# A gated attention and expert kernel: another order for the lead-in, dummy matmuls, ten halved units, and one copy on VectorE

## The chip, the cores and the metric

The kernel runs on one core of one Trainium2 chip. The metric is the device time of one execution in microseconds (us). Before the change it is 1477.9 us, the median of three runs (1477.68 to 1480.69). The engines are named TensorE (PE; its weight loads PEld), VectorE (DVE, in the code V), ScalarE (ACT, A), GpSimd (POOL, G) and SyncE (SP), which issues most transfers (DMAs).

## What is computed

A linear recurrence with a complex decay per head, then a mixture of four experts, then a two-layer block. With q, k, v, a_re, a_im of shape 4 x 8 x 768 x 48:

```
a      = (a_re, a_im) * min(|a|, 0.999) / (|a| + 1e-6)
S[t]   = a[t] * S[t-1] + k[t] v[t]^T          (complex S, 48 x 48 per head)
y[t]   = q[t] . Re S[t]
x      = y of all heads side by side           (3072 tokens x 384)
x      = sum_e p_e * (relu(x @ w1[e]) @ w2[e])  (4 experts, 384 -> 1024 -> 384)
out    = leaky_relu(x @ w_in, 0.01) @ w_out     (384 -> 2048 -> 384)
```

## The kernel before

**Chunks.** The 3072 tokens are 24 chunks of 128. For each chunk the recurrence is done in closed form. `elementwise(c)` is a generator of 17 steps on VectorE, ScalarE and GpSimd: clip, logarithms, a running sum of log magnitudes (scan), the decays, a running sum of phases (scan), its reduction, sine and cosine, and at last the features `ft` of q and k. An eighteenth call runs `by_head`, six transfers that rearrange `ft` into `hd` by head. `products(c)` is a generator on TensorE: transposes of k into `kt` (two steps, each with a copy out of PSUM), scores `sc` with the causal mask on VectorE (two steps), the state update `pm` / `st`, the output `py` in two steps of four heads with the copy `y`, and the transposes `px` of y with the split of the result into a rounded part `xh` and a rest `xl`. All of these use two PSUM buffers in turn (`ps_a`).

**Groups and units.** Four chunks are a group of 512 tokens, six groups in all. A unit is a slice of 128 hidden columns: 32 units of the experts (first stage), 16 of the last block (second stage). For each step of the list `order`, `gemm_in` does nine matmuls into `ph`, VectorE makes `hp` of it, ScalarE rounds it to `hh`, VectorE takes the rest `hl` (`split_h`), and `gemm_out` does nine matmuls into three sums `acc`. `gemm_in` runs two steps ahead of `gemm_out`. Weights of the first stage come as `raw`, are split into rounded part and rest by ScalarE and GpSimd (`split_unit`; for the first three units by `cast_early` and, on TensorE, `rest_early`), stored to memory (`ws`, L626), and loaded back for later groups (`load_split`). The second stage's weights are decoded in the background.

**Halves.** In the first group the first `NHALF` units run twice in half width: first all of them for the first 256 tokens (chunks 0 and 1), then all of them for the other 256 (chunks 2 and 3), so that matmuls can begin when two chunks are ready. A half step has 256-column matmuls.

**What sets the order.** Each engine works its instructions off in the order in which the program lists them, and so does SP with its transfers. Up to the first `gemm_in` the string `PLAN` (L35) is that order: a digit is one step of `elementwise` of that chunk, `p` and `q` are steps of `products` of chunks 0 and 1, `s` an early cast, `m` an early rest, `n` the normalised probabilities. After it `background()` (L531) lists what is left, one *tick* at a time: the rest of `elementwise` of chunks 2 and 3, `WAIT` empty ticks, `products` of chunk 2 and of chunk 3, then for each later chunk `NSTEPS` ticks, those in `PSTEPS` being steps of its `products` and the others steps of the next chunk's `elementwise`. `tick` (L581) is called twice in each step, after `gemm_in` and after `gemm_out`, and takes as many ticks as the table `pace` asks for, at most three a call. `pace` goes from 0 at the start to `first` ticks at `KN` units, and then evenly to the beginning of each group, less `MARGIN`.

**The end of a stage.** `evacuate` (L600) copies the three sums to `o`, all on ScalarE, behind the `hh` of the step after next. The first matmuls of the next `gemm_out` write the same three sums.

Of the kernel before, what the change touches and what calls it, by code (L numbers as in the profile page):

```python
# [10 lines left out]
F32 = mybir.dt.float32  # L11
# [8 lines left out]
P = 128  # L20
# [4 lines left out]
NG = DM // P  # L25
DG = 16
TG = 512
# [3 lines left out]
NU = 48  # L31
WU = 2 * DM
AR_MIN = 0.76
NHALF = 8
PLAN = (  # L35
    "0101001010101011" "01ss0000mm" "00sss11mm000" "1111ppsm23111qq"
    "23232n3pp23p2ppqq3q23qqpq23m"
)
MAXT = 3
KN = 3.0  # L40
PT = 32
TPOOL = 6
MARGIN = 2.0
LAG = 2
E2 = 20
RAWS = 4
WTS = 7
DEC = 33.0
PSTEPS = (1, 3, 5, 12, 14, 17, 20, 22, 24)
ESTEPS = 17  # L50
LOADSTEP = 9
NSTEPS = ESTEPS + len(PSTEPS)
WAIT = 4
AR_MAX = 1e4
AI_MAX = 1.0
PI = 3.1415925
# [5 lines left out]
def fused_kernel(  # L62
# [13 lines left out]
    V, A, G, SP, PE = nc.vector, nc.scalar, nc.gpsimd, nc.sync, nc.tensor  # L76
# [6 lines left out]
    with ExitStack() as fast:  # L83
# [74 lines left out]
        def table(name):  # L158
            if tables[0] != name:
                A.preload_act_table_set(name)  # L160
                tables[0] = name

        def elementwise(c):
            t, vt = inputs[c]
            ar, ai, q, k = (t[:, i] for i in range(4))
# [77 lines left out]
        def by_head(c):  # L243

            ft, vt = feats[c]
            pool = p_el2 if c in (1, 3) else p_el
            hd = pool.tile([2 * D, H, 2 * P + 1], F32, name="hd")
            for ri in range(2):
                for i in range(NG):
                    row = ri * D + i * DG  # L250
                    (A if c < 2 and (i == ri or i == 2 - ri) else SP).dma_start(hd[row : row + DG], ft[:, ri, i])
            feats[c] = (ft, hd, vt)


# [3 lines left out]
        def products(c):  # L258
            if c >= CPG:
                by_head(c)  # L260
                yield
            ft, hd, vt = feats.pop(c)
            pool = p_el2 if c in (1, 3) else p_at
            first = c % NCH == 0
            kt = pool.tile([P, H, 2 * D], F32, name="kt", bufs=1)
            for ri in range(2):
                pt = ps_a.tile([P, NG, P], F32, name="pt", tag="pa")
                for i in range(NG):
                    PE.transpose(pt[:, i], ft[:, ri, i, P : 2 * P], ident)  # L269
                A.copy(  # L270
                    kt[:, :, ri * D : (ri + 1) * D].rearrange("t h (r d) -> t r d h", d=DG),
                    pt.rearrange("t r (d h) -> t r d h", h=H),
                )
                yield
            att = pool.tile([P, H, P], F32, name="att", bufs=1)
            for hh in range(2):
                sc = ps_a.tile([P, 4, P], F32, name="sc", tag="pa")
                for j in range(4):
                    h = 4 * hh + j
                    PE.matmul(sc[:, j], hd[:, h, P : 2 * P], hd[:, h, :P], start=True, stop=True)  # L280
                V.tensor_tensor(
                    att[:, 4 * hh : 4 * hh + 4], sc, causal[:, None].to_broadcast([P, 4, P]), ALU.mult
                )
                yield
            old = state.pop(c, None)
            if (c + 1) % NCH:
                pm = ps_a.tile([2 * D, H, D], F32, name="pm", tag="pa")
                for h in range(H):
                    PE.matmul(pm[:, h], kt[:, h], vt[:, h * D : (h + 1) * D], start=True, stop=True)  # L289
                st = p_at.tile([2 * D, H, D], F32, name="st")  # L290
                decay = hd[:, :, 2 * P :].to_broadcast([2 * D, H, D])
                if first:
                    V.tensor_tensor(st, pm, decay, ALU.mult)
                else:
                    V.tensor_tensor(st, pm, old, ALU.add)
                    V.tensor_tensor(st, st, decay, ALU.mult)
                state[c + 1] = st
                yield
            py = ps_a.tile([P, H, D], F32, name="py", tag="pa")
            for h in range(H):  # L300
                PE.matmul(py[:, h], att[:, h], vt[:, h * D : (h + 1) * D], start=True, stop=first)  # L301
                if not first:
                    PE.matmul(py[:, h], hd[:, h, :P], old[:, h], start=False, stop=True)  # L303
                if h == 3:
                    yield
            y = pool.tile([P, DM], F32, name="y", bufs=1)
            A.copy(y, py.rearrange("t h e -> t (h e)"))
            yield
            px = ps_a.tile([P, NG, P], F32, name="px", tag="pa")
            for i in range(NG):  # L310
                PE.transpose(px[:, i], y[:, i * P : (i + 1) * P], ident)  # L311
            grp, j = divmod(c, CPG)
            if j == 0:
                xg[grp] = (
                    p_x.tile([P, NG, TG], F32R, name="xh"),
                    p_x.tile([P, NG, TG], F32R, name="xl"),
                )
            xh, xl = (x[:, :, j * P : (j + 1) * P] for x in xg[grp])
            A.copy(xh, px)
            V.tensor_tensor(xl, px, xh.bitcast(F32), ALU.subtract)  # L320
            yield
# [164 lines left out]
                PE.matmul(out, wt[:, 0, cols], hl, start=False, stop=last)  # L486


        def zipped(*gens):
            gens = list(gens)  # L490
            while gens:
                for x in list(gens):
                    if next(x, gens) is gens:
                        gens.remove(x)
                yield

        def run_all(*gens):
            gens = list(gens)
            while gens:
                gens = [x for x in gens if next(x, gens) is not gens]  # L500

        with tc.manual_schedule():
            table("natural_log_exp_and_others")
            load_chunk(0, 0)
# [9 lines left out]
            steps = {str(c): elementwise(c) for c in range(CPG)}  # L514
            steps.update(zip("pqrt", (products(c) for c in range(CPG))))
            early_halves = iter([(s, part) for s in range(6) for part in (0, 1)][: PLAN.count("s")])
            for x in PLAN + "m" * 8:
                if x in steps:
                    next(steps[x], None)
                elif x == "n":  # L520
                    normalise_probs()
                    load_pb(0)
                elif x == "s":
                    cast_early(*next(early_halves))
                elif x == "m":
                    rest_early()
            for s in (5, 6):
                load_unit(s)
            split_unit(3, 0)

            def background():  # L531
                for _ in range(2):
                    next(steps["2"])
                    yield
                for _ in zipped(steps["2"], steps["3"]):
                    yield
                load_chunk(4)
                for _ in range(WAIT):
# [32 lines left out]

            dec = decoding()

            first = 2 + max(0, ESTEPS + 1 - min(PLAN.count("2"), PLAN.count("3"))) + WAIT + E2 - PLAN.count("r") - PLAN.count("t")
            pace = [(0.0, 0), (KN, first)]
            for g in range(1, NGRP):
                pace.append((begins[g] - MARGIN, first + ESTEPS + (NSTEPS + 1) * CPG * g))
# [22 lines left out]
            def evacuate(acc):  # L600

                out = [pools["x2"].tile([P, TG], F32, name="o", bufs=NG) for _ in acc]
                for o, a in zip(out, acc):
                    A.copy(o, a)  # L604
                return out

            acc = None
# [235 lines left out]
```

## Time and profile before

| what | value |
|---|---|
| median of three runs | 1477.9 us |
| the profiled execution | 1478.36 us |
| its span | 1476.6 us |
| TensorE busy | 1402.4 us, 95% |
| VectorE busy | 864.7 us, 59% |
| ScalarE busy | 564.8 us, 38% |
| mean granted clock of TensorE over the execution | 0.976 |

The profile records one execution. Busy time is the time in which an engine had an instruction at work. The granted clock is 1.0 for TensorE's full clock and 0.5 for half. In lists in order of time, the bracket at the end of a line gives the idle time of the engine before it and what ended that time.

### The profile page before, as it was taken

The page shows a single profiled execution, that of the slowest core. Times are in us where ns is not written, and L with a number is a line of the kernel's source. Part 1 is how long each engine was busy: PE and PEld are TensorE (multiplying, and loading weights), DVE is VectorE, ACT ScalarE, POOL GpSimd, SP SyncE. Part 2 cuts the span into 40 slices and gives each one's busy share as a digit, 9 for nine tenths or more (in the row PEclk, how much of TensorE's full clock was granted, in tenths as well). Part 3 has the DMA queues.
Part 4 walks back from the last instruction along what each step waited for, and adds up shares of the span by engine and source line. Part 5 has one row for each costly group of instructions (what it writes and reads, how often), then busy time and mean ns, then how long its engine had stood idle before and what let it go on. Part 6 is the DMA issues. An engine that isn't in the chain of part 4 may idle for free.

```text
span 1476.6 us, 18540 instructions
## 1 busy us (share of the span) xinstructions
PE 1402.4 (95%) x6978; PEld 1177.2 (80%) x6978; DVE 864.7 (59%) x1504; ACT 564.8 (38%) x961; POOL 264.5 (18%) x244
## 2 busy tenths in 40 slices
PE   3858999999999999999999999999999999999997
PEld 1858888888777888788888888888888888888886
DVE  7556887788988898785454554554443333333332
ACT  5424565444345434455234354233332111323232
POOL 2120565412223223221011110110110000100000
PEclk9569999999999999999999999999999999999999
DMA  7288789986788789588567477576465665556561
GB/s 192 43 207 301 212 255 298 331 291 208 273 301 290 250 305 319 153 303 245 153 234 222 151 242 216 188 222 199 154 199 172 231 207 196 190 188 208 190 212 65
DMA packets 91043, 325.49 MB, mean 220 GB/s; under 512 B 10464, under 2 KB 32064, under 8 KB 90944
## 3 DMA queue, kind: packets, MB, share of 16 engines
q1 hardware_dynamic: 87488, 318.71, 67.1%
q10 hardware_dynamic: 3456, 5.51, 1.3%
q8 instruction: 56, 0.92, 0.3%
q14 instruction: 43, 0.35, 0.1%
HBM read 262.72 MB, written 42.52 MB: 207 GB/s over the span
## 4 chain that ended last, share of the span: by engine, by line
PE 58%; DVE 2%; ACT 0%; issue 0%; DVEq 0%; ACTq 0%
PE ph L455 27%; PE acc L484 9%; PE acc L486 9%; PE acc L485 9%; PE sc L280 1%; PE py L301 1%; PE py L303 1%; PE pm L289 1%; PE pt L269 0%; DVE hl L473 0%; DVE hp L460 0%; PE px L311 0%; DVE d L349 0%; ACT hh L472 0%; DVE d L355 0%
## 5 line engine op out<-in xcount | busy, mean ns | idle before, releaser
L455 PE MATMUL ph<-xh,wt 128*128 128x512 f32 (+1 forms) x1200 | 397.9, 388 | 0.0
L484 PE MATMUL acc<-hh,wt 128*128 128x512 f32 (+1 forms) x888 | 350.8, 395 | 5.2 <-ACT o L604 5.1
L486 PE MATMUL acc<-hl,wt 128*128 128x512 f32 (+1 forms) x888 | 342.9, 386 | 4.5 <-DVE hl L473 4.5
L485 PE MATMUL acc<-hh,wt 128*128 128x512 f32 (+1 forms) x888 | 341.5, 385 | 0.0
L472 ACT CAST hh<-hp 128x512 fp32r<-128x512 f32 (+1 forms) x296 | 180.4, 610 | 418.2 <-DVE hp L460 326.5
L473 DVE TENSOR_TENSOR hl<-hp,hh 128x512 fp32r<-128x512 f32 (+1 forms) x296 | 213.4, 721 | 150.3 <-ACT hh L472 149.1
L455 PEld LDWEIGHTS ph<-xh,wt 128*128 128x128 f32 x1200 | 225.5, 190 | 42.4 <-ACT ge L121 0.3
L460 DVE SCALAR_TENSOR_TENSOR hp<-ph,pb 128x512 f32<-128x512 f32 (+1 forms) x200 | 133.0, 665 | 189.9 <-PE ph L455 188.6
L455 PE MATMUL ph<-xl,wt 128*128 128x512 f32 (+1 forms) x600 | 230.2, 384 | 0.0
L486 PEld LDWEIGHTS acc<-hl,wt 128*128 128x128 f32 x888 | 167.3, 188 | 40.0 <-DVE hl L473 6.0
L455 PE MATMUL ph<-x2h,wt 128*128 128x512 f32 x576 | 198.3, 398 | 0.0
L484 PEld LDWEIGHTS acc<-hh,wt 128*128 128x128 f32 x888 | 167.7, 189 | 36.5 <-ACT o L604 5.8
L485 PEld LDWEIGHTS acc<-hh,wt 128*128 128x128 f32 x888 | 168.0, 189 | 30.7
L463 DVE SCALAR_TENSOR_TENSOR hp<-hp 128x512 f32<-128x512 f32 x96 | 72.0, 750 | 185.0 <-ACT hp L462 184.9
L455 PEld LDWEIGHTS ph<-xl,wt 128*128 128x128 f32 x600 | 114.1, 190 | 20.3 <-DVE xl L320 0.2
L455 PEld LDWEIGHTS ph<-x2h,wt 128*128 128x128 f32 x576 | 108.7, 189 | 25.1
L462 ACT COPY hp<-ph 128x512 f32<-128x512 f32 x96 | 56.3, 586 | 178.5 <-PE ph L455 178.5
L455 PE MATMUL ph<-x2l,wt 128*128 128x512 f32 x288 | 114.5, 397 | 0.0
L409 POOL TENSOR_TENSOR wt<-raw,wt 128x384 fp32r<-128x384 f32 x58 | 65.0, 1142 | 62.4 <-ACT wt L408 62.3
L643 POOL TENSOR_TENSOR x2l<-o,x2h 128x512 fp32r<-128x512 f32 x18 | 25.2, 1424 | 256.4 <-ACT x2h L642 256.4
L301 PE MATMUL py<-vt,att 128*128 128x48 f32 x384 | 70.9, 280 | 0.1
L280 PEld LDWEIGHTS sc<-hd 96*128 96x128 f32 x384 | 54.2, 208 | 15.4 <-issue 7.9
(97 smaller groups left out, 1482.2 us busy)
## 6 DMA issues: line engine op xcount, KB each, us to landing
wt<-ws_scratch SPq DMA_DIRECT2D x264, 768.0 KB, 4.8
ws_scratch<-wt SPq DMA_DIRECT2D x32, 768.0 KB, 7.5
hd<-ft SPq DMA_DIRECT2D x138, 128.5 KB, 5.4
aaqk<-in_attn_dram SPq DMA_DIRECT2D x22, 768.0 KB, 8.9
raw<-in_w_dram SPq DMA_DIRECT2D x32, 384.0 KB, 4.5
r<-in_w_dram SPq DMA_DIRECT2D x32, 384.0 KB, 7.4
ws_scratch<-dw SPq DMA_DIRECT2D x32, 384.0 KB, 6.2
pb<-pn_scratch SPq DMA_DIRECT2D x24, 256.0 KB, 6.5
```

Source lines behind the costliest of these rows:

```text
L280: PE.matmul(sc[:, j], hd[:, h, P : 2 * P], hd[:, h, :P], start=True, stop=True)
L301: PE.matmul(py[:, h], att[:, h], vt[:, h * D : (h + 1) * D], start=True, stop=first)
L409: G.tensor_tensor(wt[:, 1], raw, wt[:, 0].bitcast(F32), ALU.subtract)
L455: PE.matmul(ph[:, : t1 - t0], wt[:, wi, cols], x[kc][:, t0:t1], start=n == 0, stop=n == 3 * NG - 1)
L460: V.scalar_tensor_tensor(hp, ph, 0.0, pbs[g, u // 8][:, t0:t1], ALU.max, ALU.mult)
L462: A.copy(hp, ph)
L463: V.scalar_tensor_tensor(hp, hp, 0.01, hp, ALU.mult, ALU.max)
L472: A.copy(hh, hp)
L473: V.tensor_tensor(hl, hp, hh.bitcast(F32), ALU.subtract)
L484: PE.matmul(out, wt[:, 0, cols], hh, start=first, stop=False)
L485: PE.matmul(out, wt[:, 1, cols], hh, start=False, stop=False)
L486: PE.matmul(out, wt[:, 0, cols], hl, start=False, stop=last)
```

## The change

`PLAN` has another order from its fourth part on, without the eight `m` at its end, and with the letter `w`: three dummy matmuls (`warm`) of 384 columns into the bank of the first sum, read by nobody. `products` of chunk 1 has four more dummies among the heads of `py`, and its `kt` is copied by VectorE. Chunk 1's `by_head` is issued by SP alone. `NHALF` is 10 for 8. The steps of chunks 2 and 3 that are left follow the string `LATER`, one to a tick, chunk 2 first; `WAIT` is 11, `KN` 4, and `first` follows from these (48 ticks, before 36). In `PSTEPS` the steps of `py` come one tick earlier and `px` one later, in the last tick of its chunk. In `evacuate` VectorE copies the middle sum.

```
--- before.py
+++ after.py
@@ -31,26 +31,27 @@
 NU = 48
 WU = 2 * DM
 AR_MIN = 0.76
-NHALF = 8
+NHALF = 10
 PLAN = (
-    "0101001010101011" "01ss0000mm" "00sss11mm000" "1111ppsm23111qq"
-    "23232n3pp23p2ppqq3q23qqpq23m"
+    "0101001010101011" "01ss0000mm" "00sss11mm000" "1111ppsmww23111"
+    "23n22qqw33ppm22p3ppmqqw3q2233qqpq"
 )
+LATER = "23222232232223333333"
 MAXT = 3
-KN = 3.0
+KN = 4.0
 PT = 32
 TPOOL = 6
 MARGIN = 2.0
 LAG = 2
-E2 = 20
+E2 = 17
 RAWS = 4
 WTS = 7
 DEC = 33.0
-PSTEPS = (1, 3, 5, 12, 14, 17, 20, 22, 24)
+PSTEPS = (1, 3, 5, 12, 14, 17, 19, 21, 25)
 ESTEPS = 17
 LOADSTEP = 9
 NSTEPS = ESTEPS + len(PSTEPS)
-WAIT = 4
+WAIT = 11
 AR_MAX = 1e4
 AI_MAX = 1.0
 PI = 3.1415925
@@ -160,6 +161,15 @@
                 A.preload_act_table_set(name)
                 tables[0] = name
 
+        def warm(n):
+
+            out = ps_acc.tile([P, TG], F32, name="warm", tag="acc0")
+            for _ in range(n):
+                PE.matmul(
+                    out[:, : NG * P], ident, inputs[0][0][:, 0].rearrange("p g t -> p (g t)"),
+                    start=True, stop=True,
+                )
+
         def elementwise(c):
             t, vt = inputs[c]
             ar, ai, q, k = (t[:, i] for i in range(4))
@@ -248,7 +258,7 @@
             for ri in range(2):
                 for i in range(NG):
                     row = ri * D + i * DG
-                    (A if c < 2 and (i == ri or i == 2 - ri) else SP).dma_start(hd[row : row + DG], ft[:, ri, i])
+                    (A if c == 0 and (i == ri or i == 2 - ri) else SP).dma_start(hd[row : row + DG], ft[:, ri, i])
             feats[c] = (ft, hd, vt)
 
 
@@ -267,7 +277,7 @@
                 pt = ps_a.tile([P, NG, P], F32, name="pt", tag="pa")
                 for i in range(NG):
                     PE.transpose(pt[:, i], ft[:, ri, i, P : 2 * P], ident)
-                A.copy(
+                (V.tensor_copy if c == 1 else A.copy)(
                     kt[:, :, ri * D : (ri + 1) * D].rearrange("t h (r d) -> t r d h", d=DG),
                     pt.rearrange("t r (d h) -> t r d h", h=H),
                 )
@@ -301,6 +311,8 @@
                 PE.matmul(py[:, h], att[:, h], vt[:, h * D : (h + 1) * D], start=True, stop=first)
                 if not first:
                     PE.matmul(py[:, h], hd[:, h, :P], old[:, h], start=False, stop=True)
+                if c == 1 and h % 2:
+                    warm(1)
                 if h == 3:
                     yield
             y = pool.tile([P, DM], F32, name="y", bufs=1)
@@ -486,19 +498,6 @@
                 PE.matmul(out, wt[:, 0, cols], hl, start=False, stop=last)
 
 
-        def zipped(*gens):
...
-        def run_all(*gens):
...
         with tc.manual_schedule():
             table("natural_log_exp_and_others")
             load_chunk(0, 0)
@@ -514,7 +513,7 @@
             steps = {str(c): elementwise(c) for c in range(CPG)}
             steps.update(zip("pqrt", (products(c) for c in range(CPG))))
             early_halves = iter([(s, part) for s in range(6) for part in (0, 1)][: PLAN.count("s")])
-            for x in PLAN + "m" * 8:
+            for x in PLAN:
                 if x in steps:
                     next(steps[x], None)
                 elif x == "n":
@@ -524,15 +523,15 @@
                     cast_early(*next(early_halves))
                 elif x == "m":
                     rest_early()
+                elif x == "w":
+                    warm(3)
             for s in (5, 6):
                 load_unit(s)
             split_unit(3, 0)
 
             def background():
-                for _ in range(2):
-                    next(steps["2"])
-                    yield
-                for _ in zipped(steps["2"], steps["3"]):
+                for x in LATER:
+                    next(steps[x], None)
                     yield
                 load_chunk(4)
                 for _ in range(WAIT):
@@ -571,7 +570,7 @@
 
             dec = decoding()
 
-            first = 2 + max(0, ESTEPS + 1 - min(PLAN.count("2"), PLAN.count("3"))) + WAIT + E2 - PLAN.count("r") - PLAN.count("t")
+            first = len(LATER) + WAIT + E2
             pace = [(0.0, 0), (KN, first)]
             for g in range(1, NGRP):
                 pace.append((begins[g] - MARGIN, first + ESTEPS + (NSTEPS + 1) * CPG * g))
@@ -600,8 +599,8 @@
             def evacuate(acc):
 
                 out = [pools["x2"].tile([P, TG], F32, name="o", bufs=NG) for _ in acc]
-                for o, a in zip(out, acc):
-                    A.copy(o, a)
+                for i, (o, a) in enumerate(zip(out, acc)):
+                    (V.tensor_copy if i == 1 else A.copy)(o, a)
                 return out
 
             acc = None
```

## Rows read from the trace of the kernel before

**Rows 1.** The profile page, its head.

```profile
span 1476.6 us, 18540 instructions
```

**Rows 2.** Busy time by stretches: us, then the columns of the head line.

```profile
core 0: us, PE busy (x) PEld busy (x) DVE busy (x) ACT busy (x) POOL busy (x), PEclk, DMA share, GB/s
...
44.47:66.66 22.19, 22.19 (x105) 21.04 (x106) 9.22 (x20) 4.06 (x8) 0.00 (x0) 0.50 0.08 30
...
66.74:128.01 61.27, 43.46 (x310) 42.00 (x309) 34.62 (x65) 20.99 (x41) 15.10 (x14) 0.81 0.75 225
...
128.01:285.00 156.99, 149.11 (x839) 127.69 (x838) 124.95 (x204) 86.97 (x156) 80.54 (x72) 0.99 0.87 268
...
320.00:600.00 280.00, 272.15 (x1391) 227.85 (x1390) 249.43 (x454) 120.99 (x204) 73.11 (x65) 1.00 0.81 279
```

**Rows 3.** TensorE in order of time: start us, us, engine, line, operation, tiles.

```profile
27.70 0.81 PE L429 MATMUL ph<-raw,ident 128*128 128x384 f32 x2
...
50.48 3.75 PE L280 MATMUL sc<-hd 96*128 96x128 f32 x16
...
54.02 2.69 PE L289 MATMUL pm<-vt,kt 128*96 128x48 f32 x16
...
66.74 0.58 PE L455 MATMUL ph<-xh,wt 128*128 128x256 f32 x1
...
95.70 0.55 PE L280 MATMUL sc<-hd 96*128 96x128 f32 x1 [5.40 <-DMA hd<-ft]
...
116.64 0.39 PE L301 MATMUL py<-vt,att 128*128 128x48 f32 x2
...
118.41 0.36 PE L455 MATMUL ph<-xh,wt 128*128 128x256 f32 x1
...
122.01 0.55 PE L311 MATMUL px<-ident,y 128*128 128x128 f32 x3 [0.57 <-ACT y L307]
...
125.85 0.28 PE L455 MATMUL ph<-xh,wt 128*128 128x256 f32 x1
...
128.01 0.28 PE L455 MATMUL ph<-xh,wt 128*128 128x256 f32 x1
```

**Rows 4.** Single microseconds in which the granted clock (third from the end) changed.

```profile
66.00:67.00 1.00, 1.00 (x4) 0.53 (x2) 1.00 (x5) 0.54 (x2) 0.00 (x0) 0.66 0.00 0
...
107.00:108.00 1.00, 0.68 (x7) 0.55 (x5) 0.00 (x0) 0.29 (x1) 0.00 (x0) 0.82 1.04 430
```

**Rows 5.** VectorE's share of two stretches, and single instructions in order of time.

```profile
32.68:47.85 15.17, 8.68 (x42) 8.02 (x43) 7.86 (x21) 7.90 (x13) 0.00 (x0) 0.50 0.70 97
...
71.74:86.72 14.98, 4.42 (x35) 4.00 (x33) 14.70 (x28) 6.86 (x14) 6.63 (x7) 0.79 0.35 132
...
35.61 1.45 ACT L270 COPY kt<-pt 128x384 f32<-128x384 f32 x2 [3.16 <-issue]
...
55.45 1.06 DVE L198 TENSOR_TENSOR_SCAN tb<-ones,ta 128x128 f32<-128x128 f32 x3
...
64.74 0.56 DVE L320 TENSOR_TENSOR xl<-px,xh 128x384 fp32r<-128x384 f32 x1 [6.86 <-ACT xh L319]
```

**Rows 6.** Issues of the head transfers, on ScalarE's queue and on SP's.

```profile
32.80 2.77 ACTq L251 DMA_DIRECT2D hd<-ft  x3
...
86.75 7.71 SPq L251 DMA_DIRECT2D hd<-ft  x12
```

**Rows 7.** The chain that ended last, a late piece: start us, us, what.

```profile
1434.23 2.10 PE ph L455 x9
```

**Rows 8.** Transfers: DMA share and GB/s, last two columns, of three stretches.

```profile
92.00:93.00 1.00, 0.00 (x0) 0.00 (x0) 0.02 (x1) 1.00 (x3) 0.00 (x0) 1.00 1.18 121
...
106.00:107.00 1.00, 1.00 (x11) 1.00 (x10) 0.00 (x0) 0.00 (x0) 0.00 (x0) 1.00 1.05 442
...
320.00:325.00 5.00, 5.00 (x26) 4.16 (x25) 3.78 (x7) 3.80 (x7) 1.99 (x2) 1.00 1.07 253
```

**Rows 9.** TensorE's waits from 320 to 700 us: total us, times, longest.

```profile
PE px L311 <- ACT y L307: 5.2, 3, 2.4
...
PE acc L484 <- ACT o L604: 5.1, 2, 3.3
```

More of the change, by code (lines that the diff above doesn't have):

```diff
@@ L33 @@
 AR_MIN = 0.76
-NHALF = 8
+NHALF = 10
 PLAN = (
-    "0101001010101011" "01ss0000mm" "00sss11mm000" "1111ppsm23111qq"
-    "23232n3pp23p2ppqq3q23qqpq23m"
+    "0101001010101011" "01ss0000mm" "00sss11mm000" "1111ppsmww23111"
+    "23n22qqw33ppm22p3ppmqqw3q2233qqpq"
 )
+LATER = "23222232232223333333"
 MAXT = 3
-KN = 3.0
+KN = 4.0
 PT = 32
@@ L44 @@
 LAG = 2
-E2 = 20
+E2 = 17
 RAWS = 4
@@ L52 @@
 NSTEPS = ESTEPS + len(PSTEPS)
-WAIT = 4
+WAIT = 11
 AR_MAX = 1e4
@@ L161, in table, with warm @@
                 tables[0] = name
+        def warm(n):
+            out = ps_acc.tile([P, TG], F32, name="warm", tag="acc0")
+            for _ in range(n):
+                PE.matmul(
+                    out[:, : NG * P], ident, inputs[0][0][:, 0].rearrange("p g t -> p (g t)"),
+                    start=True, stop=True,
+                )
         def elementwise(c):
@@ L250, in by_head @@
                     row = ri * D + i * DG
-                    (A if c < 2 and (i == ri or i == 2 - ri) else SP).dma_start(hd[row : row + DG], ft[:, ri, i])
+                    (A if c == 0 and (i == ri or i == 2 - ri) else SP).dma_start(hd[row : row + DG], ft[:, ri, i])
             feats[c] = (ft, hd, vt)
@@ L269, in products @@
                     PE.transpose(pt[:, i], ft[:, ri, i, P : 2 * P], ident)
-                A.copy(
+                (V.tensor_copy if c == 1 else A.copy)(
                     kt[:, :, ri * D : (ri + 1) * D].rearrange("t h (r d) -> t r d h", d=DG),
@@ L303, in products @@
                     PE.matmul(py[:, h], hd[:, h, :P], old[:, h], start=False, stop=True)
+                if c == 1 and h % 2:
+                    warm(1)
                 if h == 3:
@@ L486, in gemm_out @@
                 PE.matmul(out, wt[:, 0, cols], hl, start=False, stop=last)
[L489 to L500, printed above, removed]
         with tc.manual_schedule():
@@ L516, in fused_kernel @@
             early_halves = iter([(s, part) for s in range(6) for part in (0, 1)][: PLAN.count("s")])
-            for x in PLAN + "m" * 8:
+            for x in PLAN:
                 if x in steps:
@@ L526, in fused_kernel @@
                     rest_early()
+                elif x == "w":
+                    warm(3)
             for s in (5, 6):
@@ L531, in background @@
             def background():
[L532 to L535, printed above, removed]
+                for x in LATER:
+                    next(steps[x], None)
                     yield
@@ L572, in fused_kernel @@
             dec = decoding()
-            first = 2 + max(0, ESTEPS + 1 - min(PLAN.count("2"), PLAN.count("3"))) + WAIT + E2 - PLAN.count("r") - PLAN.count("t")
+            first = len(LATER) + WAIT + E2
             pace = [(0.0, 0), (KN, first)]
@@ L602, in evacuate @@
                 out = [pools["x2"].tile([P, TG], F32, name="o", bufs=NG) for _ in acc]
-                for o, a in zip(out, acc):
-                    A.copy(o, a)
+                for i, (o, a) in enumerate(zip(out, acc)):
+                    (V.tensor_copy if i == 1 else A.copy)(o, a)
                 return out
```

2 lines of the change are left out of this document (1 added, 1 removed).

## The prediction

> **What bounds the kernel now.** I read the page first: a span of 1476.6 us inside an execution of 1478.36, so 1.8 us lie around the span [rows 1]. Then the busy time by stretches [rows 2]. From 128 us on TensorE (PE) works 149.1 of 157.0 us, and from 320 to 600 it works 272.2 of 280: there the run is a queue of matmuls, with VectorE (V) not far behind (249.4 of 280). The lead-in is another thing: from 66.74 to 128.01 PE works 43.5 of 61.3 us at a mean granted clock of 0.81, and from 44.47 to 66.66 it works all the time, 22.19 of 22.19, at 0.50. So the loss to look for is in the first 128 us, as idle time and as half clock. PE's order in time [rows 3] gives the marks: the first GEMM matmul at 66.74, the scores of chunk 2 at 95.70, the eleventh `gemm_in` at 128.01 (two before it, 125.85: a half step costs 2.16 at full clock). I call these G, S and X. What comes after X is the same PE work in both kernels, but for the two more units that are halved; so the change is worth what it moves X, plus what it does to stalls behind X.
>
> **The clock, as the rows have it.** Two levels, 1.0 and 0.5 (2.4 and 1.2 GHz). It rose in the 67th microsecond, when four 384-column rest passes had run, and fell in the 108th, right after `py` of chunk 2, whose matmuls are 48 columns wide [rows 4]. The dummies of the change are 384-column passes of the kind that took 0.81 for two, 0.65 from start to start [rows 3]: one dummy (two passes) is 0.65 at full clock and 1.3 at half. There are 16.
> The Trainium skill ("TensorE: Matmul & The Clock Gate", section "Why this matters for your kernels") advises to keep TensorE busy without gaps to have the full clock. By that alone the stretch from 44.47 should have been full, and it was at 0.50 without a gap: the trace does not agree for these narrow matmuls. What the rule would make of the time is the second rival.
>
> **Part 1, up to G.** `ww` follows the rest passes, which end by 29.2 (0.81 from 27.70 and as much again for the other operand), and takes 3.9 us; chunk 1's features, PE's next work, are ready at 32.80, when their transfers go out [rows 3, 6]. It hides, and costs 0.3 at most. The next `w` lies behind `kt` of chunk 1, where PE has to wait for V's copies of it anyway. These two copies leave ScalarE (1.45 us for two, after 3.16 us of idle time while it issued) for V: between 0.56 each, V's reading of as many PSUM numbers, and 0.87, ScalarE's own time; I take 0.7, 1.4 for two [rows 5]. The three head transfers of chunk 1 that ScalarE issued took its queue 2.77 us; on SP, at about 0.64 each as in the twelve that took 7.71, they end 1.9 us later [rows 6], and chunk 1's scores are not due for another 8 us: nothing.
> Scores of chunk 1 (50.48 today) need a PSUM buffer that V frees with chunk 0's state. From 32.68 to 47.85, its end, V works only 7.86 us [rows 5]; the new order puts in the two copies (1.4) and chunk 2's next scan step (1.6, of which 1.06 the scans), and I add 1.3 for two exponentials that come behind the last rest copy on ScalarE (0 to the 7.3 that V idles there today). 32.68 + 7.86 + 1.4 + 1.6 + 1.3 = 44.9. From there PE has, one after the other [rows 3]: scores 3.75 (half clock, since only narrow work came before), `w` 3.9 at half clock, which should bring the clock up, then at full clock `pm` 1.35 (half of 2.69), `py` 3.55 (1.77 from 116.64 to 118.41 for four heads), four dummies between its heads 2.6, and 1.8 for the copy of y, its transposes and the cast (0.57 idle and 0.55, and about 0.7). The last two rest passes no longer stand here. G = 61.9, against 66.74. All at full clock it would be 58.1; all at half, 70.5, later than today: the four dummies stand on the path.
>
> **Part 2, from G to S.** Today this is 28.96 us and V sets it: from 71.74 to 86.72 it works 14.70 of 14.98 [rows 5]. The new order takes chunk 2 first, and so leaves out three steps of chunk 3 before chunk 2's transfers (six passes, some 2.1 us by the 0.56 of a whole pass), but adds one `hl` (0.4) and a wait for ScalarE's sine and cosine (1.3): 0.4 gained, 28.6, S = 90.5. Chunk 2's transfers then take the 8.95 that lie between 86.75 and 95.70 today. With WAIT at 11 and a step at a time, three more `gemm_in` and two more `gemm_out` lie ahead of S; V's `hp` and `hl` for them fill the time of the transfers.
>
> **Part 3, from S to X.** Today 32.31 us. Five halves of half steps are gone, three at 1.08 and two at 2.16 (half clock): 7.5. Scores and `pm` of chunk 2 run at half clock today (3.75, and 2.69 like chunk 1's, a little overlapped); PE now comes to them from dense 256-column work, so 3.0 less. 21.8 are left, to which I add 1.7 for one more fall after chunk 2's `py`, which still stands unbroken. X = 61.9 + 28.6 + 23.5 = 114.0: 14.0 earlier. Two more halved units: nine whole matmuls take 2.10 [rows 7], eighteen halves 2.16, so 4 x 0.06 = 0.24 back.
>
> **Part 4, transfers.** From chunk 2's issue (81.5) to the fifth reload's use at X + 4 x 2.16 = 122.6 there are 41.1 us. In them go, with sizes by the tiles' shapes, two sets of head transfers (0.79 MB each, 121 GB/s while they run: 13.2 with their start), and at about 430 GB/s (442 in a bulk microsecond) eight stores and five reloads of 0.786 MB and two chunk loads of 0.98: 12.2 MB, 28.4 [rows 8]. 41.6 against 41.1: it is full. I take 1.0 of stall.
>
> **Part 5, the rest.** From 320 to 700 PE waits 5.2 us for y before `px` and 5.1 for ScalarE's first copy of a sum [rows 9]. The last transposes now come four ticks behind y instead of two, about half a unit more of matmuls, so most of the 5.2 goes there; but V and ScalarE are near a step behind PE in this stretch, and half may come back at `hl`: I take 2.6 (0 to 5.2). The waits for the sum are for the *first* copy, which stays where it was, behind `hh` on ScalarE; V's copy of the middle one (0.56 to 0.7) waits behind `hl` and holds up only the next `hp`, which has not been computed yet. Nothing, within 0.5 either way, and so at the end of the run.
>
> Sum: -14.0 + 0.24 + 1.0 - 2.6 = -15.4 against the execution's 1478.36: **1463.0**. That execution stands 0.5 above the median of the runs, 1477.9, which I leave within the error.
>
> **Rivals.**
> *The dummies don't hold the clock* (G = 70.5, all narrow work at 0.5). For it: 22 us of narrow work at 0.50; against: passes like them came before the rise at 66.66. 8.6 later: 1471.6.
> *Any gapless work has the full clock*, the skill's rule above as a mechanism of this kernel: G = 58.1 and no fall behind chunk 2's `py`, 3.8 + 1.7 less: 1457.5. Against it stand the rows of 44.47 to 66.66 and of 107 to 108.
> *V gives it back.* From X to 600 V works 80 to 89% of the time, and 125 background ticks now have 26 units instead of 27. If V can't take the denser order, one unit (4.2) and the 2.6 of part 5 are lost: 1469.8.
> *Slower: the transfers become the pace of the second half steps.* Ten units are stored and reloaded instead of eight, and the sum of part 4 has no slack. Where small-packet transfers mixed with bulk, a stretch of 5 us at full DMA share moved 253 GB/s [rows 8]; at that rate the 12.2 MB take 48.2, 19.8 more, and the reloads come so much late: 1482. It decides below about 275 GB/s, where the extra reaches 15.4. Against it: the same kinds of transfers moved 442 in a microsecond of today's lead-in.
>
> **How the numbers follow.** The sum as it stands, 1463: 0.50. Full clock on any work, 1457.5: 0.13. No clock from the dummies, 1471.6: 0.14. V gives back, 1469.8: 0.12. Transfers, 1482: 0.06. Two of the losses together, near today's time: 0.05. A measurement of this kernel tells about 0.2%, 3 us, from no change. Faster, then, 0.89; same 0.05; slower 0.06. The range of 8 in 10 takes in the first four cases with the bounds of G (58.1 to 70.5) and of part 5: 1453 to 1474.
>
> **What would show it.** G near 62 and X near 114 on PE, the clock at 1.0 in chunk 1's `py`, no wait of `px` for y in the third stage, and a PE that never waits for a reload. Wrong would be: a half clock between 52 and 60; waits of `ph` for a DMA between 115 and 130; idle time of PE from X to 285 above today's 7.9; or the stall before `acc` gone, which I hold to be untouched.

## The result: slower by 0.6%, and the profile after

The kernel after takes 1489.61 us, the median of ten runs (1483.66 to 1492.62), beside 1481.22 for the kernel before on the same chips (ten runs, 1476.91 to 1483.56): a ratio of 1.0059 [1.0041, 1.0077]. Forecast were 1463 and a range of 1453 to 1474. The profiled execution, 1492.62 with a span of 1490.9, is the slowest of the ten; its mean granted clock is 0.975, and the median over the ten is 0.977.

First TensorE's marks, in order of time (columns as in [rows 3]): the dummies, the scores of chunk 1, G, the scores of chunk 2 (S), and X, the eleventh `gemm_in`.

```profile
29.42 4.36 PE L168 MATMUL warm<-aaqk,ident 128*128 128x384 f32 x12
...
44.43 2.05 PE L290 MATMUL sc<-hd 96*128 96x128 f32 x16 [0.57 <-ACT y L319]
...
57.23 0.38 PE L467 MATMUL ph<-xh,wt 128*128 128x256 f32 x1 [0.62 <-ACT xh L331]
...
99.59 3.78 PE L290 MATMUL sc<-hd 96*128 96x128 f32 x16 [12.37 <-ACT kt L280]
...
132.43 0.38 PE L467 MATMUL ph<-xh,wt 128*128 128x256 f32 x1 [0.57 <-ACT xh L331]
```

G came 9.5 us earlier than in [rows 3]. S came 3.9 later and X 4.4 later. So all of the gain at G, and more, was lost between G and S, and the line of S says how: TensorE waits 12.37 us for ScalarE's copy of `kt`. ScalarE in order of time shows what it was doing:

```profile
84.85 0.40 ACT L484 CAST hh<-hp 128x256 fp32r<-128x256 f32 x1 [1.60 <-DVE hp L472]
97.90 0.92 ACT L420 CAST wt<-raw 128x384 fp32r<-128x384 f32 x2 [12.64 <-DMA ws_scratch<-wt]
98.73 1.48 ACT L280 COPY kt<-pt 128x384 f32<-128x384 f32 x2
```

The cast at 97.90 is `split_unit` for the tenth unit (number 9). It waits 12.64 us for a transfer, a store of a unit to `ws`, and the two copies that TensorE needs stand behind it in ScalarE's queue. The reason lies in the ring of seven `wt` buffers. Units 0 to 6 take them once; 7 and 8 take those of units 0 and 1. In step 5 `load_split(s + 5)` asks for the first reload ahead of `split_unit(s + 4, 0)`, so the reload gets unit 2's buffer and unit 9 gets unit 3's, which is free only when unit 3 has been stored. SP's queue shows when that was (issues in order of time):

```profile
77.50 3.79 SPq L261 DMA_DIRECT2D hd<-ft  x6
81.34 0.60 SPq L625 DMA_DIRECT2D ws_scratch<-wt  x1
83.35 3.78 SPq L261 DMA_DIRECT2D hd<-ft  x6
87.22 0.55 SPq L151 DMA_DIRECT2D aaqk<-in_attn_dram  x1
87.92 0.33 SPq L155 DMA_DIRECT2D vt<-in_v_dram  x1
89.05 1.33 SPq L625 DMA_DIRECT2D ws_scratch<-wt  x2
91.03 0.34 SPq L412 DMA_DIRECT2D wt<-ws_scratch  x1
```

Unit 2 is stored at 81.34, and the stores of units 3 and 4 stand behind chunk 3's six head transfers and chunk 4's load, at 89.05. In the kernel before, SP issued these twelve head transfers only at 86.75 [rows 6], behind the stores that its last splits needed, and no cast waited for a store.

Then the clock. Stretches as in [rows 2]; the third figure from the end is the granted clock:

```profile
43.90:57.23 13.33, 12.18 (x84) 10.01 (x84) 8.52 (x19) 4.11 (x9) 2.34 (x2) 1.00 0.22 79
57.23:99.59 42.36, 22.24 (x132) 20.14 (x132) 25.73 (x43) 13.44 (x29) 16.19 (x15) 0.77 0.75 197
90.00:91.00 1.00, 0.00 (x0) 0.00 (x0) 0.00 (x0) 0.00 (x0) 0.00 (x0) 0.53 1.15 136
99.59:132.43 32.84, 30.88 (x176) 29.95 (x176) 7.50 (x15) 5.35 (x12) 1.84 (x2) 0.63 0.64 225
124.00:125.00 1.00, 1.00 (x11) 1.00 (x11) 0.17 (x1) 0.41 (x1) 0.00 (x0) 0.91 0.71 230
132.43:299.80 167.37, 156.46 (x873) 133.84 (x874) 123.25 (x210) 88.26 (x158) 76.73 (x67) 0.96 0.81 251
320.00:600.00 280.00, 274.40 (x1387) 230.39 (x1386) 249.26 (x453) 122.40 (x207) 70.74 (x63) 0.99 0.83 278
299.80:1490.90 1191.10, 1173.66 (x5681) 978.96 (x5679) 676.42 (x1162) 419.13 (x697) 161.77 (x139) 0.99 0.67 219
```

In the stretch that was at 0.50 without a gap in [rows 2], the clock is now 1.00. Behind G it is at 0.50 twice for a short time (73 to 76 and 80 to 86 us), each time after TensorE had idled for some microseconds. In the long wait it falls again, in the 91st microsecond, and returns only in the 125th, though TensorE is busy for 30.88 of the 32.84 us from S to X. So the wait is paid twice, as idle time and as half clock behind it.

The time between X and the end of the first stage (the first copy of a sum, 285.7 before and 299.8 after) grew from 157.7 to 167.4 us; TensorE is busy 156.46 of it, 149.81 before. From there to the end of the span it is 1191.1. In the kernel before, both stretches (the first row has TensorE's columns alone):

```profile
128.01:285.70 157.69, 149.81 (x842) 0.99 0.87 269
285.70:1476.60 1190.90, 1170.60 (x5677) 975.88 (x5676) 662.93 (x1148) 424.45 (x707) 158.71 (x138) 1.00 0.67 219
```

TensorE's waits after X (to 299.8), and from 320 to 700, beside [rows 9]:

```profile
PE sc L290 <- DMA hd<-ft: 7.2, 3, 3.9
```

```profile
PE py L311 <- DVE att L291: 2.6, 2, 1.5
PE px L323 <- ACT y L319: 2.4, 2, 1.9
PE acc L496 <- ACT o L603: 2.3, 1, 2.3
```

The wait of scores for head transfers was 1.5 us in the same stage before. `px` waits less for y, as forecast, but `py`, a tick earlier now, waits 2.6 for `att`. The wait for the copy of a sum, which the prediction held to be untouched, fell from 5.1 to 2.3.

### The profile page after: what moved, and what is told of

Read it like the earlier page. It is cut to its first block, busy times and chain, and to the rows that moved or that the text cites. A ratio compares the mean times of both kernels' runs of the same rounds, so it can differ in the third digit from the quotient of the medians.

```text
span 1490.9 us, 18674 instructions
## 1 busy us (share of the span) xinstructions
PE 1419.1 (95%) x7046; PEld 1187.7 (80%) x7046; DVE 877.5 (59%) x1522; ACT 557.3 (37%) x949; POOL 269.0 (18%) x244
## 4 chain that ended last, share of the span: by engine, by line
PE 66%; DVE 20%; ACT 7%; DMA 3%; issue 2%; SPq 1%; POOL 0%; ACTq 0%; DVEq 0%
PE ph L467 28%; PE acc L496 10%; PE acc L498 9%; PE acc L497 9%; DVE hl L485 3%; PE sc L290 2%; PE py L311 2%; DVE hp L472 2%; PE py L313 2%; ACT hh L484 2%; DMA hd<-ft 2%; DVE ft L244 2%; PE pm L299 1%; DVE d L366 1%; DVE th L226 1%
## 5 line engine op out<-in xcount | busy, mean ns | idle before, releaser
L496 PE MATMUL acc<-hh,wt 128*128 128x512 f32 (+1 forms) x894 | 356.2, 398 | 8.8 <-ACT hh L484 6.4
L497 PE MATMUL acc<-hh,wt 128*128 128x512 f32 (+1 forms) x894 | 344.9, 386 | 0.0
L485 DVE TENSOR_TENSOR hl<-hp,hh 128x512 fp32r<-128x512 f32 (+1 forms) x298 | 218.5, 733 | 159.8 <-ACT hh L484 157.2
L467 PEld LDWEIGHTS ph<-xh,wt 128*128 128x128 f32 x1212 | 229.1, 192 | 46.0 <-ACT xh L331 2.5
L496 PEld LDWEIGHTS acc<-hh,wt 128*128 128x128 f32 x894 | 170.4, 191 | 40.1 <-ACT hh L484 7.6
L498 PEld LDWEIGHTS acc<-hl,wt 128*128 128x128 f32 x894 | 170.3, 190 | 38.9 <-DVE hl L485 4.7
L497 PEld LDWEIGHTS acc<-hh,wt 128*128 128x128 f32 x894 | 170.8, 191 | 29.8
L290 PE MATMUL sc<-hd 96*128 96x128 f32 x384 | 56.3, 296 | 21.4 <-ACT kt L280 12.6
```

What stands on the lines that cost most here:

```text
L467: PE.matmul(ph[:, : t1 - t0], wt[:, wi, cols], x[kc][:, t0:t1], start=n == 0, stop=n == 3 * NG - 1)
L485: V.tensor_tensor(hl, hp, hh.bitcast(F32), ALU.subtract)
L496: PE.matmul(out, wt[:, 0, cols], hh, start=first, stop=False)
L497: PE.matmul(out, wt[:, 1, cols], hh, start=False, stop=False)
```

## The experiments

Theory: the loss is the ring of buffers, a wait that ten units bring and that the dummies have no part in. Rivals: the dummies cost somewhere; ten units cost by their transfers' bandwidth; or the steps late in the run (part 5) cost. Ratios are to the kernel before on the same chip, with a 95% interval.

**Taking the change apart: e1_dummies_eight.** The new `PLAN` with its dummies, chunk 1's `kt` on VectorE and its heads on SP, but eight units, the old background, the old late steps and all copies of sums on ScalarE. Cut from its difference to the kernel after:

```
-NHALF = 10
+NHALF = 8
...
-KN = 4.0
+KN = 3.0
...
-PSTEPS = (1, 3, 5, 12, 14, 17, 19, 21, 25)
+PSTEPS = (1, 3, 5, 12, 14, 17, 20, 22, 24)
...
-WAIT = 11
+WAIT = 4
```

> The new order up to the first GEMM matmul with its dummies, chunk 1's copies on VectorE and its transfers on SP; but eight halved units, the old background, old PSTEPS, old copies of the sums. Theory A (the loss comes from the ten units: unit 9's split on ScalarE waits for the buffer that the store of unit 3 frees, and that store is issued behind chunk 3's transfers and chunk 4's load): without ten units no such wait; the first GEMM matmul near 57 as in the changed kernel, and 5 to 10 us faster than the kernel before. Rival B (the dummies and the new order are themselves the loss, through the clock or through VectorE): no faster, 0 to +8 us. Rival C (the tick positions and the middle copy lose it in the stages): also faster here, told from A by the runs of those parts alone.

Measured: 1473.71 us, 0.9952 [0.9937, 0.9967]. G 57.40. No wait of ScalarE for a store; chunk 2's scores wait for their own transfers only:

```profile
86.22 3.76 PE L289 MATMUL sc<-hd 96*128 96x128 f32 x16 [5.42 <-DMA hd<-ft]
```

The dummies and the new order ahead of G are a gain of 0.5%; the loss is in the rest.

**e2_ten_alone.** The kernel before with ten units and the background that belongs to them (`LATER`, `WAIT` 11, `KN` 4, `E2` 17); no dummies, old late steps. Cut from its difference to the kernel before:

```
-NHALF = 8
+NHALF = 10
...
+LATER = "23222232232223333333"
```

> Ten halved units with their background (LATER, WAIT 11, KN 4, E2 17), but the old order up to the first GEMM matmul, no dummies, old PSTEPS, old copies of the sums. Theory A: the wait of ScalarE for a store in the lead-in is there, 8 us or more, and the kernel is 8 to 20 us slower than before, since it has the loss and not the earlier start. Rivals B and C: within 4 us of before.

Measured: 1497.42, 1.0105 [1.0085, 1.0125]. ScalarE's waits from 60 to 135:

```profile
ACT wt L418 <- DMA ws_scratch<-wt: 12.7, 1, 12.7
```

The same wait without a dummy. Ten units, as they stand, lose about 1%.

**Taking the wait away: e4_later_reload.** The kernel after, with the reloads of the halved units asked for four steps ahead instead of five, so that unit 9's split gets unit 2's buffer, stored 7.7 us earlier.

```
-                load_split(s + 5)
+                if s <= NHALF:
+                    load_split(s + 4)
+                if s >= NHALF:
+                    load_split(s + 5)
```

> The changed kernel with the reloads of the halved units taken four steps ahead instead of five, so that unit 9's split gets the buffer of unit 2, whose store is issued some 8 us before unit 3's. Theory A: ScalarE's longest wait for a store falls from 12.6 to 6 us or less, the eleventh gemm_in comes 6 to 10 us earlier, and the time is 5 to 12 us below the changed kernel's. Rival D (the transfers as a whole bind): the wait only moves to a reload, and the time stays within 3 us of the changed kernel's.

Measured: 1477.9, 0.9976 [0.9963, 0.999]. ScalarE's wait, and TensorE at S and X:

```profile
ACT wt L420 <- DMA ws_scratch<-wt: 2.8, 1, 2.8
```

```profile
89.50 2.90 PE L290 MATMUL sc<-hd 96*128 96x128 f32 x16 [3.77 <-ACT kt L280]
...
116.16 0.38 PE L467 MATMUL ph<-xh,wt 128*128 128x256 f32 x1 [0.57 <-ACT xh L331]
```

X is 16.3 us earlier than in the kernel after. The 308 matmuls from G to X take 45.95 us of TensorE's time where they took 53.11: of the 16.0 us that this stretch is shorter, 8.9 are idle time and 7.2 busy time, which at the same matmuls is half clock that came with the wait. Theory A held. But even with the wait at 2.8 us the ten units are no better than the eight of e1_dummies_eight: 0.9976 beside 0.9952, on the same chip. The medians are 11.7 apart; the stretch behind X differs too (below), and the profiled executions are the slowest of ten and the fastest of twelve.

**e3_kt2_vector.** The kernel after, with chunk 2's `kt` copied by VectorE: it takes the copies out of the blocked queue and leaves the wait.

```
-                (V.tensor_copy if c == 1 else A.copy)(
+                (V.tensor_copy if c in (1, 2) else A.copy)(
```

> The changed kernel with the copies of kt of chunk 2 on VectorE as well. Theory A: ScalarE still stands some 12 us for the store, but TensorE gets to chunk 2's scores when their transfers have landed, near 87, runs scores, pm and py, and waits later, for y on ScalarE; 3 to 8 us faster than the changed kernel. Rival D (it is the transfers themselves that bind, chunk 2's have not landed before 97): scores still not before 97, no gain.

Measured: 1487.89, 1.0041 [1.0026, 1.0055]. S comes at 89.58 and at full clock, but ScalarE still waits 12.8 us. TensorE's longest waits from 60 to 135:

```profile
PE pm L299 <- DVE att L291: 10.9, 1, 10.9
PE acc L496 <- ACT hh L484: 5.7, 2, 3.7
```

The wait went one step on: `hh` is behind the cast on ScalarE, `hl` behind `hh`, and chunk 2's `att` behind `hl` on VectorE. The gain on the kernel after, 0.18% or some 2.7 us by the two ratios, lies within their intervals. A blocked queue isn't mended by taking one instruction out of it.

**Why the store is late: e17_store_on_scalar.** The kernel after, with the stores of the first five units issued by ScalarE. The ring is as it was.

```
-                    SP.dma_start(ws[u], wts[s].bitcast(F32))
+                    (A if s < 5 else SP).dma_start(ws[u], wts[s].bitcast(F32))
```

> The kernel after, with the stores of the first five units issued by ScalarE in place of SP. In the kernel after, SP issues unit 3's store at 89.05, behind twelve head transfers and chunk 4's load, and it lands at 97.9. Theory A, SP's order makes it late: ScalarE issues it near 80, it lands by 90, ScalarE's wait falls from 12.6 to under 6 us, TensorE's before chunk 2's scores from 12.4 to under 7, and the kernel comes to 0.997 to 1.002 of before. Theory B, the full DMA engines make it late whoever issues it: it lands after 94, the wait stays above 9 us, and the kernel stays near 1.006.

Measured: 1478.08, 0.9974 [0.9954, 0.9993]. ScalarE and its issues in order of time:

```profile
81.70 0.34 ACTq L625 DMA_DIRECT2D ws_scratch<-wt  x1
...
84.54 0.34 ACTq L625 DMA_DIRECT2D ws_scratch<-wt  x1
86.82 0.93 ACT L420 CAST wt<-raw 128x384 fp32r<-128x384 f32 x2 [1.90 <-DMA ws_scratch<-wt]
```

The head transfers of chunks 2 and 3, which SP issues in the same run:

```profile
77.15 15.23 SPq L261 DMA_DIRECT2D hd<-ft  x12
```

The store of unit 3 goes out at 81.70, in the middle of the same head transfers, and ScalarE goes on at 86.82. So SP's order made it late, as Theory A said. Of the 11.1 us by which the cast comes earlier, 7.4 are the earlier issue; the other 3.7 are a shorter way from the store's issue to the cast, 5.1 us for 8.9, and what made that way shorter, no run shows (in the kernel after, chunk 4's load goes out just ahead of the store). The Trainium skill ("DMA: Bandwidth & Descriptors", section "Issuing engines are not separate DMA queues", and its rules for kernel authors) says that transfers from all engines share the same DMA engines and interleave, and that issuing them from several engines only saves issue time, which is usually small beside the transfer. The trace agrees on the first: the store was done within 5.1 us of its issue, amid SP's twelve head transfers. The saving was not small here: the issue came 7.4 us earlier, since what stood ahead of the store on SP no longer did, and by the two ratios this edit was worth 0.85% of the run.

**e15_ten_alone_later_reload.** e2_ten_alone with e4's edit.

> The ten units and their background without dummies, as in e2_ten_alone, with the later first reload. If ScalarE's wait for the store is what the ten units cost, the 12.7 us there goes to about 3 and most of e2_ten_alone's 1.05% over before goes with it: 0.995 to 1.002 of before. Rival: ten units cost by their transfers or by the denser background, and over 0.5% stays.

Measured: 1488.17, 1.0046 [1.0031, 1.0061]. ScalarE's wait falls from 12.7 to 2.7 us, and somewhat more than half of the 1.05% goes. Neither expectation holds in full: 0.5% stays. In the kept trace X is 5.1 us earlier than before the change, but X to the end of the stage takes 160.6 us for 157.7, and the rest 1195.2 for 1190.9. That execution is the fastest of ten (1480.48, clock 0.977; the median clock is 0.970), so where the others lose more isn't shown.

**The clock between S and X: e10_dummies_chunk2.** e4_later_reload with six more dummies of 384 columns in front of chunk 2's scores, in a buffer of `ph`.

```
+            if c == 2:
+                warm(6, ps_h, 2)
```

> The later first reload of e4_later_reload, with six more dummy matmuls of 384 columns in the 3.8 us in which TensorE waits before chunk 2's scores. In e4_later_reload the clock falls to 0.5 at 90.25, just as the scores begin, and stays there until 97.2 with TensorE busy throughout. Theory A: dummies in the gap hold the clock, scores, pm and the next gemm_in take half the time, and the kernel gains 2 to 3.5 us. Theory B: TensorE's pace isn't what the end waits for (VectorE and the transfers are), or the narrow work makes the clock fall all the same: within 1 us of e4_later_reload.

Measured: 1473.44, 0.9942 [0.9929, 0.9955], against 0.9976 for e4_later_reload. TensorE in e4_later_reload, in the 11.5 us from its S on, and in e10_dummies_chunk2 around its own (us, busy, clock, DMA share, GB/s):

```profile
89.50:101.00 11.50, 11.18 (x73) 0.69 1.06 326
```

```profile
88.00:101.00 13.00, 13.00 (x95) 0.98 1.06 299
```

Theory A of this run held. By the ratios the gain is 0.34%, 5 us, more than the 2 to 3.5 expected, but the intervals allow 2 to 8; in the two traces the stretch from G to X is 2.3 us shorter (56.87 for 59.16).

**Part 5 alone: e6_psteps_alone and e7_evac_alone.** The kernel before with the new `PSTEPS`, and with VectorE's copy of the middle sum.

```
-PSTEPS = (1, 3, 5, 12, 14, 17, 20, 22, 24)
+PSTEPS = (1, 3, 5, 12, 14, 17, 19, 21, 25)
```

> The kernel before, with the new PSTEPS alone. The prediction took -2.6 us for this (between 0 and -5.2). Theory A, that neither this nor the middle copy does anything: within 1.5 us of before, because from the first copy of a sum to the end the kernels before and after took 1190.9 and 1191.1. Theory B, that the two cancel: -2.6 here and +2.6 for the middle copy alone. Under both the waits of px for y behind 320 us should fall from 5.2 to below 3.

> The kernel before, with VectorE's copy of the middle sum alone. The prediction took 0 within 0.5. Theory A: within 1.5 us of before. Theory B, that it costs what the other steps of py and px give: +2.6. The wait of acc for o behind 320 us, 5.1 before, should fall under both, since the three copies then end sooner.

Measured: 1484.25, 1.0012 [1.0001, 1.0023], and 1482.94, 1.0008 [0.9999, 1.0016]. Both lie within the 0.2%: in the kernel with eight units part 5 doesn't bring its 2.6 us, and the new steps and the middle copy don't cancel each other. In e6_psteps_alone the wait of `px` for y is gone altogether. TensorE there, from the first copy of a sum to the end, beside the same row of before above:

```profile
292.90:1487.10 1194.20, 1177.41 (x5678) 982.22 (x5676) 669.10 (x1148) 424.62 (x707) 162.78 (x138) 0.99 0.67 218
```

Idle time fell from 20.3 to 16.8 us (the length of the stretch less TensorE's busy time), and busy time for the same matmuls rose from 1170.6 to 1177.4, so the stretch got 3.3 us longer. This trace is of the slowest of twelve executions, and e1 and e7, with the old steps, have 1172.1 and 1172.4 busy in stretches of 1190.7 and 1191.2: part of the rise is scatter. In the kernel after the two move by 2.9 and 3.1.

**A version to beat both: e9_three_mends.** e4_later_reload, chunk 2's `kt` on VectorE, and chunk 4's load nine empty ticks later.

```
-                load_chunk(4)
-                for _ in range(WAIT):
+                for k in range(WAIT):
+                    if k == 9:
+                        load_chunk(4)
```

> The later first reload of e4_later_reload, with chunk 2's kt copies on VectorE too and chunk 4's inputs loaded nine empty ticks later. If what is left of the loss is ScalarE's 2.8 us wait for a store and the 3.77 that chunk 2's scores wait for ScalarE, the two go: 2 to 5 us below e4_later_reload, 1473 to 1476, no worse than e1_dummies_eight. Rival: VectorE or the transfers have the pace there (the DMA share is at 1 from 84 to 118 us), and it stays within 1.5 us of e4_later_reload.

Measured: 1469.73, 0.9923 [0.991, 0.9936], the lowest ratio of all versions, and 0.53% below e4_later_reload, more than the 2 to 5 us expected. S and X:

```profile
87.68 2.05 PE L290 MATMUL sc<-hd 96*128 96x128 f32 x16 [0.36 <-DVE kt L280]
...
112.35 0.38 PE L467 MATMUL ph<-xh,wt 128*128 128x256 f32 x1 [0.57 <-ACT xh L331]
```

ScalarE still waits 2.7 us for a store, but chunk 2's scores wait only 0.36. X is 20 us earlier than in the kernel after and near the 114.0 of the prediction; that it is so near is in part luck, since G is 4.6 earlier than forecast and G to X 3.0 longer. The 308 matmuls from G take 43.80 us. Eight units with the two further edits were not run, so it isn't shown that ten are better than eight.

**e11_mends_dummies.** e9_three_mends with e10's six dummies.

> e9_three_mends with the six dummies of e10_dummies_chunk2. Theory A, the clock is worth its time there: another 2 to 5 us, 1465 to 1468. Theory B: TensorE waits only 1 us before these scores in e9_three_mends, so the 2 us of dummies stand on its path and give back what the clock brings: within 1.5 us of e9_three_mends, or slower by up to 2.

Measured: 1472.23, 0.9935 [0.9917, 0.9954]: no gain over e9_three_mends. In e9 TensorE waits 0.36 us at S and its scores run at full clock already; the dummies of e10 filled a gap that is no longer there. Theory B held.

**e12_mends_old_tail.** e9_three_mends with the old `PSTEPS` and all copies of sums on ScalarE.

> e9_three_mends with the old PSTEPS and all three copies of the sums on ScalarE. Each of the two was 0.08 to 0.12% slower alone, in the kernel before. Theory A, that they are worth nothing, but for scatter: within 1.5 us of e9_three_mends. Theory B, that they cost what e6 and e7 show: 2 to 3 us faster, 1467. The prediction's part 5: 2.6 slower.

Measured: 1471.57, 0.993 [0.9911, 0.9948]: the same as e9_three_mends. `px` again waits 6.1 us for y between 320 and 700 us. That the total is the same hides two differences. From the first copy of a sum to the end (TensorE's columns alone), e9_three_mends and then this run:

```profile
276.80:1468.00 1191.20, 1173.84 (x5681) 0.99 0.68 219
```

```profile
274.80:1469.80 1195.00, 1172.87 (x5680) 1.00 0.67 219
```

Behind that first copy the new late steps and copies save 3.8 us; from X up to it they cost 3.3 (164.45 us in e9, 161.2 in this run). Other traces agree on the first: behind the first stage the three with ten units and old steps (e2, e12, e15) take 1194.8 to 1195.2 us, the seven with ten units and new steps (the kernel after, e3, e4, e9, e10, e11, e17) 1191.0 to 1191.4. With eight units it is the other way round: 1190.7 to 1191.2 with the old steps (before, e1, e7), 1194.2 with the new (e6). So ten units cost some 4 us there, which the new steps give back. From X to the copy, old steps with ten units take 160.6 to 161.6 us and new ones 161.3 to 167.4.

**e14_earlier_heads.** e9_three_mends, with the head transfers a step earlier and the scores a step later.

```
+PSTEPS = (0, 3, 5, 13, 15, 18, 20, 22, 25)
```

> e9_three_mends with other steps for products: the head transfers in the first step of a chunk instead of its second, and the scores, with what follows but px, one step later. In e9_three_mends scores wait 7.2 us for head transfers between 135 and 300 us, as in the kernel after, with the clock at 0.91 from 200 to 240. Theory A: the waits end the time there; they fall below 2 us, the clock stays at 1.0, and the kernel gains 4 to 9 us. Theory B: VectorE or the transfers' rate set the pace, and the wait shows up elsewhere: within 1.5 us of e9_three_mends.

Measured: 1474.79, 0.9952 [0.9935, 0.9969]: slower than e9_three_mends, where 4 to 9 us of gain were expected. The wait for head transfers fell from 7.2 to 0.2 us. The stage from X to its end, first in e9_three_mends, then in e14_earlier_heads (us, TensorE busy, clock, DMA share, GB/s):

```profile
112.35:276.80 164.45, 153.22 (x873) 0.98 0.86 269
```

```profile
113.35:280.80 167.45, 159.52 (x873) 0.94 0.84 264
```

For the same 873 matmuls TensorE idles 7.9 us in place of 11.2, and is busy 6.3 longer at a lower clock. Behind the stage another 3.9 us are lost (1195.1 for 1191.2). The trace is of the slowest of the six. Over six runs the mean clock is 0.979 to 0.985, where the five of e9 have 0.985 to 0.988. Theory A named the wait rightly and failed on the gain, since the clock took more than the wait gave; theory B, that nothing would move, failed as well.

## Why the prediction was wrong, point by point

**Part 1 (G 61.9; it was 57.23): right in kind, too small.** The clock didn't have to be brought up again, since it never fell ahead of G: chunk 1's scores took 2.05 us and the `w` behind them 2.10, where 3.75 and 3.9 had been put down. That is 3.5 of the 4.7. The rival in which the dummies don't hold the clock is out. No run has the new order without the dummies, so what the dummies did alone, beside the four rest passes that moved in among the narrow work, is argued and not shown.

**Part 2 and 3 (S 90.5, X 114.0; they were 99.59 and 132.43): this is the step that failed.** "Chunk 2's transfers then take the 8.95" was the only wait that the sum had ahead of S. In fact the transfers went out early enough (77.50), and S waited for ScalarE, which stood at a cast without a buffer. The prediction counted the ten units' matmuls, and their stores and reloads as bytes; it never asked which buffer the first reload and the tenth split get, nor what stands ahead of the store that frees it. Measured, from G to S: 42.36 us for 28.6; with the wait at 2.8 us 32.50 (e4) and, with `kt` on VectorE and a later load, 30.41 (e9). From S to X: 32.84 for 23.5, and 24.67 in e9. The 3.0 us that part 3 took off for chunk 2's scores and `pm` at full clock failed with it: behind the wait they took 3.78 and 2.69, at half clock. In all, parts 2 and 3 had 52.1 us and the kernel after took 75.20; the edit to the ring alone (e4) brings that to 59.16, so most of the error is that wait, and with two more edits it is 55.08 (e9). What the other 7 us of e4 are is shown only as far as e9 takes them away.

**Part 4 (1.0 of stall).** The sum weighed the right transfers against the wrong instruction. TensorE never waited for a reload in the kernel after, as forecast, and with the same transfers and another order of issue most of the wait was gone (e17: 1.9 us for 12.6). The rival that ended on the slow side, transfers as the pace of the second half steps, had the size about right (19.8 us, where X came 18.4 later than forecast) and the place wrong: that is luck. That the time behind X would stay as it was, but for 1.24 us, also failed: X to the end of the stage took 9.7 us longer, 3.0 of them idle and 6.7 busy time at a lower clock (0.96 for 0.99). With the mends it is still 3.6 (e17) to 6.8 (e9) longer than before. The wait for head transfers is in that time, but taking it away (e14) didn't bring it back. The new late steps, which order this stage too, have some 3 us of it (e12 beside e9); what sets the clock there stays open.

**Part 5 (-2.6): 0.** `px` waited less for y, and TensorE's idle time behind the first stage fell by 2.9 us, but no median gained (e6, e12). The sum priced the late steps from 320 to 700 us alone. Behind the first stage they do save 3.8 us with ten units, but that gives back what the ten units cost there, and in the first stage, which the sum left out, they cost 3.3 (e12 beside e9). These figures are of single executions. The middle copy's cost of nothing was right (e7).

**In sum**, against 1463.0 the profiled execution, 3 us above the median, has 18.4 us more at X, 8.4 more from X to the end of the stage, and 2.8 more behind it: 29.6. V giving back the denser order wasn't seen: VectorE works 249.26 us from 320 to 600, 249.43 before.

The Trainium skill ("TensorE: Matmul & The Clock Gate", section "Why this matters for your kernels") also warns of idle gaps between bursts of matmuls. This case bears that out: the clock fell in the wait ahead of S (in the 91st microsecond), and ahead of S in e10, where dummies filled the wait, it stayed at 1.0. What the section says of steady work, that it brings the full clock, again did not hold for narrow and 256-column work from S on: of 24.5 us TensorE was busy for 23.7, at 0.50.

## What to carry to other kernels

Where a change adds turns to a ring of buffers, write down which old tile each new one displaces and which transfer or reader frees it, and then everything that stands ahead of that transfer on the engine that issues it; a bandwidth sum doesn't see it. A wait in the middle of a full-clock stretch can cost more than its length, and what one stage gains can be lost in another: compare each stage by its own length, with TensorE's busy time for the same number of matmuls beside its idle time. When a bundle of edits loses, measure its halves: here one half was worth 0.5%, the other lost 1%, and three small edits turned the whole into a gain of 0.8%.

## What the runs showed that was not expected

- The granted clock was 1.0 ahead of chunk 1's work in both kernels. Before, it fell in the 33rd microsecond, with TensorE busy for 1.25 us of the five from 28 on, and narrow work ran at 0.50 until 66. With 32 dummy passes of 384 columns (some 11 us) and four rest passes ahead of and among that work it stayed at 1.0 until 73 us.
- Less idle time of TensorE was not always less time: in the traces of e6, e14 and, behind its first stage, the kernel after 2.9 to 3.5 us of idle time went and 3.1 to 6.8 us of busy time for the same matmuls came. Each of the three traces is of the slowest execution of its kernel, and behind the first stage e9 has 4.8 us less idle time than e12 for 1.0 more of busy time.
- VectorE's copy of a 128x512 sum takes 0.684 us, ScalarE's 0.586. At the end of the first stage the three copies take 1.43 us from first start to last end when shared, 1.56 on ScalarE alone: when shared, the last copy on ScalarE waits 0.16 us for its own matmuls.
